# Probabilities times values in plain float32, each head in its own half of the array's columns

## Chip, cores and metric

One core of one Trainium2 chip runs the whole kernel as one launch. The metric is the device time of one execution in microseconds (us). Before the change it is 646.23 us, the median of three runs (646.15 to 648.87).

## What is computed

```python
def _attn_ref(q, k, v, n_sink, window):           # q, k, v: (2, 8, 768, 64) float32
    scores = scale * np.matmul(q, k.transpose(0, 1, 3, 2))
    keep = is_sink | in_window                    # key < n_sink (4), or 0 <= query - key < window (128)
    scores = np.where(keep, scores, -1e9)
    a = np.exp(scores - np.max(scores, axis=-1, keepdims=True))
    a = a / (np.sum(a, axis=-1, keepdims=True) + 1e-09)
    return np.matmul(a, v)
...
x = attn_out, heads side by side                  # (1536, 512)
h = (x @ w1) * (x @ w2) @ w3 @ w_out              # 512 -> 1024 -> 1024 -> 512
g = max(h2, 0) + alpha * min(h2, 0),  h2 = h @ w_in   # 512 -> 2048
return g @ w_out2                                 # 2048 -> 512
```

## The kernel before

Matrix products that need full precision are made from single-pass float32r matmuls: each operand is split into a high part (a float32r copy, by ScalarE) and a low part (the rest, by VectorE), and three products of parts are added. The helper is `evac_split` (lines 243 to 245). Its copy and its subtraction stand in the profile under L244 and L245 for every stage that uses it.

The program has two stretches. **Attention** goes over 8 units (batch b, pair of heads hp). One unit has two heads (e = 0, 1) and six blocks of 128 queries (i). A block needs 272 keys at most: its own 128, the 128 before it, and 16 sink columns. Per block, `stage_S` makes the scores of both heads on TensorE (L415: per head three products, each on 64 of the array's 128 rows, the two heads alternating), VectorE masks and takes the maximum (L422), ScalarE makes the exponentials and their sum (L424), VectorE inverts the sum (L426, L427), and GpSimd scales the probabilities (L429) and gathers the sink columns (L433, L435). `stage_X` transposes the probabilities on TensorE (L450, g = 0, 1, 2 has two blocks each) and evacuates them. `stage_K` does so for the sink columns (L467, L468). `stage_Tq` and `stage_Tk` transpose q and k of the next unit (L375, L384). The **feed-forward stretch** begins inside the last unit with `stage_B` (L567) and then runs to the end.

`stage_V` multiplies probabilities by values. It makes a tile of 128 rows (64 per head) by 512 queries (m = 0) or 256 queries (m = 1). Key block j gives to the queries of blocks j and j+1, so to 256 columns, or to 128 at the edge of a tile and of the sequence. Blocks 0, 1, 2 and 4 (SPLIT) have high and low parts of both operands: values in `vp` (made by GpSimd in `split_v`, L364 and L365), probabilities in `PT` (made by `evac_split`, L244 and L245). Blocks 3 and 5 (WHOLE) are plain float32, values in `vw` (loaded by two further DMAs, L359), probabilities in `PW` (L456, L459). Each head's 64 value columns stand beside 64 zero columns, so a matmul is 128 columns wide and both heads add into all 128 rows of the tile. All matmuls of `stage_V` are recorded under L498:

```python
for vt, pt in ((vp[0], th), (vp[0], tl), (vp[1], th)):                    # SPLIT: three products
    ops.append((x0 - lo_col, x1 - lo_col, vt[:, n, c], pt[:, 2 * n * P:2 * n * P + w]))
...
ops.append((x0 - lo_col, x1 - lo_col, vw[u % 2][:, n, c], PW[e][:, y0:y0 + w]))     # WHOLE: one
```

By the loops, a unit has 24 products of parts 256 wide, 6 plain products 128 wide, and 2 products with the sink values (96 rows deep, 256 wide).

The order of work on each engine comes from a scheduler. Each stage is recorded at a position (table `OFF`: for unit u, 6u plus the offset, in blocks of scores), and the scheduler then orders the engines' instructions by its own estimates. `tc.high_priority()` puts what it encloses ahead of others, and `tc.issue_after` keeps an instruction behind another one. All input DMAs are issued on SP's queue. `bank(kind="V")` is one PSUM bank, `kind="T"` three; the scores have two pairs.

Of the kernel before, what the change touches and what calls it, by code (L numbers as in the profile page):

```python
# [196 lines left out]
def kernel(  # L197
# [119 lines left out]
    SPLIT, WHOLE = (0, 1, 2, 4), (3, 5)
    vp = [at(t2, n * len(SPLIT) * 3 * D, [len(SPLIT), 3 * D]) for n in range(2)]
    vw = [at(e2, 3840 + n * len(WHOLE) * 3 * D, [len(WHOLE), 3 * D]) for n in range(2)]
    vv = [t.rearrange("p n (c d) -> p n c d", d=D)[:, :, 0:3:2, :] for t in vp]  # L320

# [16 lines left out]
    def sink_values(b):  # L338
# [6 lines left out]
        for e in range(2):  # L345
# [5 lines left out]
            for n, (nm, m) in enumerate((("q", 0), ("q", 1), ("k", 0), ("k", 1), ("v", 0)))}  # L351
# [16 lines left out]
    qT = [[at(set1, n * S, [S]) for n in range(2)], [at(t2, 2 * len(SPLIT) * 3 * D, [S]), at(t1, 0, [S])]]  # L368
# [101 lines left out]
    def stage_V(u, m, e):  # L470
        b, hp = divmod(u, NP)
        lo_col, hi_col = ((0, 512), (512, S))[m]
        if e == 0:
# [4 lines left out]
        c = slice(e * D, e * D + P)
        for j in range(NB):
            a0, a1_ = j * P, min((j + 2) * P, S)  # L480
            x0, x1 = max(a0, lo_col), min(a1_, hi_col)
            if x0 >= x1:
                continue
            w = x1 - x0
            if j in SPLIT:
                n = SPLIT.index(j)
                for vt, pt in ((vp[0], th), (vp[0], tl), (vp[1], th)):
                    ops.append((x0 - lo_col, x1 - lo_col, vt[:, n, c], pt[:, 2 * n * P:2 * n * P + w]))
            else:
                n = WHOLE.index(j)  # L490
                y0 = 2 * n * P + x0 - a0
                ops.append((x0 - lo_col, x1 - lo_col, vw[u % 2][:, n, c], PW[e][:, y0:y0 + w]))
        if e == 1:
            x0 = max(2 * P, lo_col)
            ops.append((x0 - lo_col, hi_col - lo_col, vsk[b][:, hp].rearrange("p e d -> p (e d)"),
                        skT[:, x0 - 2 * P:hi_col - 2 * P]))
        for n, (x0, x1, lt, rt) in enumerate(ops):
            nc.tensor.matmul(xp[:, x0:x1], lt, rt, start=(e == 0 and n == 0), stop=(e == 1 and n == len(ops) - 1),  # L498
                             skip_group_check=True)
        if e == 1:  # L500
            o = slice(b * S + lo_col, b * S + hi_col)
            evac_split(xh[:, hp, o], xl[:, hp, o], xp)
# [158 lines left out]
    def masks_2():  # L661
        count(cols[2][:, P:KW], 1)
        for t in vw:
            nc.gpsimd.memset(t[:, :, D:2 * D], 0.0)
        for t in vp:
            nc.gpsimd.memset(t[:, :, D:2 * D].bitcast(F32), 0.0)
# [292 lines left out]
```

## Time and profile before

| | |
|---|---|
| median of 3 runs | 646.23 us |
| the profiled execution: its own time | 648.56 us |
| its span, first to last instruction | 646.4 us |
| TensorE (PE) busy | 630.1 us, 97% of the span |
| VectorE (DVE) / ScalarE (ACT) / GpSimd (POOL) busy | 57% / 43% / 24% |
| chain that ended last, by engine | PE 81%, DVE 6%, POOL 4%, DMA 3% |
| mean granted TensorE clock | 0.99 of full speed |

PE is busy nearly everywhere, but PE's busy time counts the modelled ends of pipelined matmuls, so what one matmul costs is read from starts that follow each other, and from the chain. The other three engines do most of their work in the first 150 us: a mean over the span hides that they are nearly as full as PE there. PEld is PE's weight load.

### The profile page before, as it was taken

To read this page: it belongs to the slowest core of one execution; us is meant where nothing else is said; L and a number is where in the kernel's file an instruction comes from. 1 tells how busy PE (TensorE), PEld (TensorE's weight loads), DVE (VectorE), ACT (ScalarE), POOL (GpSimd) and SP (SyncE) were. 2 spreads that over 40 slices of the span, in tenths; PEclk is the share of its full clock that TensorE was granted. 3 is DMA by queue.
4 is the path that set the end of the run, shared out by engine and by line. 5 is a ranking of instruction groups with operands and counts; after the bars stand their busy time and mean duration, and the time that the engine had idled before them with its cause. 6 is when DMAs were issued, how large, how long until landed. Compare 5 with 4: busy or idle time off the path is not lost.

```text
span 646.4 us, 8934 instructions
## 1 busy us (share of the span) xinstructions
PE 630.1 (97%) x3194; PEld 519.8 (80%) x3194; DVE 370.8 (57%) x778; ACT 281.0 (43%) x570; POOL 153.3 (24%) x281
## 2 busy tenths in 40 slices
PE   8899998999999999999999999999999999999995
PEld 5678887888888888888888887788888888888884
DVE  7898999778995656475454778922232222322222
ACT  4788888577765443354344555411111111111110
POOL 5768767500000000000000003422222222222220
PEclk9999999899999999999999999999999999999998
DMA  6834523255451223431105334100010000100002
GB/s 140 199 83 112 117 53 92 85 184 165 161 195 66 95 101 125 137 130 66 65 16 179 131 110 152 65 0 2 0 66 0 1 1 0 66 0 1 0 1 70
DMA packets 67687, 52.23 MB, mean 81 GB/s; under 512 B 44452, under 2 KB 61108, under 8 KB 67636
## 3 DMA queue, kind: packets, MB, share of 16 engines
q1 hardware_dynamic: 67344, 51.20, 26.1%
q8 instruction: 27, 0.44, 0.3%
q10 hardware_dynamic: 292, 0.39, 0.2%
q14 instruction: 24, 0.20, 0.1%
HBM read 48.44 MB, written 3.15 MB: 80 GB/s over the span
## 4 chain that ended last, share of the span: by engine, by line
PE 81%; DVE 6%; POOL 4%; DMA 3%; issue 3%; ACT 2%; SPq 0%; POOLq 0%; ACTq 0%; DVEq 0%
PE bank L567 20%; PE bank L893 18%; PE bank L878 17%; PE bank L841 9%; PE bank L531 7%; PE bank L498 4%; PE scores L415 2%; PE bank L450 2%; DVE RAW L422 2%; POOL T L251 1%; DVE EARLY L245 1%; PE bank L519 1%; DMA EARLY<-in_k_dram 1%; DMA RAW<-in_moe_w_out_dram 1%; DMA W3T<-in_moe_w_out_dram 1%
## 5 line engine op out<-in xcount | busy, mean ns | idle before, releaser
L251 POOL TENSOR_TENSOR T<-M,T 128x512 fp32r<-128x512 f32 x48 | 65.0, 1354 | 441.0 <-ACT T L250 441.0
L567 PE MATMUL bank<-X,SET 128*128 128x512 f32 x576 | 134.9, 392 | 0.4 <-DVE lim L757 0.4
L567 PEld LDWEIGHTS bank<-X,SET 128*128 128x128 f32 x576 | 107.0, 188 | 22.2 <-PE bank L450 0.6
L880 DVE TENSOR_SCALAR M<-bank,alpha_sb 128x512 f32<-128x512 f32 x48 | 36.0, 750 | 154.0 <-PE bank L878 152.8
L250 ACT ACTIVATE T<-M 128x512 fp32r<-128x512 f32 x48 | 30.3, 631 | 179.9 <-DVE M L881 178.4
L893 PE MATMUL bank<-EARLY,T 128*128 128x512 f32 x288 | 76.2, 390 | 0.8 <-ACT T L250 0.6
L878 PE MATMUL bank<-X,EARLY 128*128 128x512 f32 x288 | 74.2, 389 | 0.0
L893 PEld LDWEIGHTS bank<-EARLY,T 128*128 128x128 f32 x288 | 53.8, 188 | 13.0 <-ACT T L250 1.0
L878 PEld LDWEIGHTS bank<-X,EARLY 128*128 128x128 f32 x288 | 54.1, 188 | 11.2
L531 PE MATMUL bank<-LATE,W3T 128*128 128x512 f32 x192 | 45.6, 391 | 0.0
L235 DVE TENSOR_SCALAR CW<-CW 128x1024 f32<-128x1024 f32 (+1 forms) x37 | 25.3, 683 | 29.5 <-ACT CW L232 29.3
L531 PEld LDWEIGHTS bank<-LATE,W3T 128*128 128x128 f32 x192 | 35.8, 188 | 7.6
L893 PE MATMUL bank<-LATE,T 128*128 128x512 f32 x144 | 40.3, 390 | 0.3 <-POOL T L251 0.3
L878 PE MATMUL bank<-X,LATE 128*128 128x512 f32 x144 | 40.1, 389 | 0.0
L237 DVE SCALAR_TENSOR_TENSOR RAW<-RAW 128x1024 int32<-128x1024 int32 x20 | 25.0, 1249 | 26.0 <-ACT RAW L234 26.0
L422 DVE CUSTOM_DVE_ANT_0 RAW<-scores,EARLY 128x272 f32<-128x272 f32 (+1 forms) x96 | 36.6, 406 | 4.6 <-PE scores L415 3.6
L498 PE MATMUL bank<-EARLY,T 128*128 128x256 f32 x192 | 37.8, 318 | 1.0 <-ACT EARLY L244 0.6
L234 ACT ACTIVATE RAW<-RAW 128x1024 int32<-128x1024 uint8 x20 | 22.8, 1141 | 31.3 <-DMA RAW<-in_moe_w_out_dram 20.4
L841 PE MATMUL bank<-EARLY,T 128*128 128x512 f32 x144 | 34.6, 389 | 0.0
L232 ACT ACTIVATE CW<-RAW 128x1024 f32<-128x1024 f32 x20 | 22.8, 1140 | 26.7 <-DMA RAW<-in_moe_w_dram 17.9
L881 DVE SCALAR_TENSOR_TENSOR M<-bank,M 128x512 f32<-128x512 f32 x48 | 33.1, 689 | 1.3
L893 PEld LDWEIGHTS bank<-LATE,T 128*128 128x128 f32 x144 | 27.0, 188 | 6.3 <-POOL T L251 0.7
(174 smaller groups left out, 1084.9 us busy)
## 6 DMA issues: line engine op xcount, KB each, us to landing
RAW<-in_moe_w_dram SPq DMA_DIRECT2D x20, 512.0 KB, 4.5
ROW<-in_moe_w_dram SPq DMA_DIRECT2D x12, 512.0 KB, 4.9
RAW<-in_moe_w_out_dram SPq DMA_DIRECT2D x12, 512.0 KB, 4.6
RAW<-in_moe_w_in_dram SPq DMA_DIRECT2D x8, 512.0 KB, 3.9
W3T<-in_moe_w_in_dram SPq DMA_DIRECT2D x8, 512.0 KB, 3.7
W3T<-in_moe_w_out_dram SPq DMA_DIRECT2D x8, 512.0 KB, 4.6
RAW<-in_v_dram SPq DMA_DIRECT2D x16, 192.0 KB, 3.6
EARLY<-in_q_dram SPq DMA_DIRECT2D x14, 192.0 KB, 3.1
```

What stands on the lines that cost most here:

```text
L235: lambda: nc.vector.tensor_scalar(c.bitcast(F32), c.bitcast(F32), -LIMIT, LIMIT, ALU.max, ALU.min),
L250: nc.scalar.activation(hi, src, AF.Copy)
L251: nc.gpsimd.tensor_tensor(lo, src, hi.bitcast(F32), ALU.subtract)
L422: st["max", u, i] = nc.vector.tensor_tensor_reduce(sm[:, :w], ps[e][:, :w], masks[:, min(i, 2), SW - w:SW], -scale, 3.0e38, ALU.add, ALU.m ...
L498: nc.tensor.matmul(xp[:, x0:x1], lt, rt, start=(e == 0 and n == 0), stop=(e == 1 and n == len(ops) - 1), skip_group_check=True)
L531: nc.tensor.matmul(ps, l[:, c, :], rt[c], start=(n == 0), stop=(n == len(mm) - 1))
L567: nc.tensor.matmul(ps, l[:, n0 + c, :], r[:, c, o], start=(n == 0), stop=(n == len(mm) - 1))
L841: nc.tensor.matmul(ps, W(c, l)[:, m * P:(m + 1) * P], ab(c, t, r), start=(n == 0), stop=(n == len(mm) - 1))
L878: nc.tensor.matmul(ps, l[:, 0, c * P:(c + 1) * P], r[:, c, o], start=(m == 0), stop=(m == len(mm) - 1))
L880: nc.vector.tensor_scalar(g, ps, 0.0, alpha_sb[:, j:j + 1], ALU.min, ALU.mult)
L881: nc.vector.scalar_tensor_tensor(g, ps, 0.0, g, ALU.max, ALU.add)
L893: st["E"] = nc.tensor.matmul(acc[t][m], l[:, o], r[:, 1, :], start=(j == 0 and x == 0), stop=(j == KF2 - 1 and x == 2)).ins
```

## The change

`stage_V` now uses plain float32 for every key block. Head 0 writes rows 0 to 63 of the tile and head 1 rows 64 to 127, with 64 value columns as weights straight from the loaded values, and the heads' matmuls alternate. The sink product, all 128 columns wide, comes first and alone carries `start`. The probabilities' transposes are copied once, head 0's by ScalarE and head 1's by VectorE. `split_v`, `vp`, `vw`, `PW`, their zeroing and the second value loads are gone. The values of odd units have a place of their own (`EARLY2`), those of even units stay in `RAW`. The block is recorded under `high_priority` with each matmul behind the one before it.

```diff
     def load(u, nm, src):
         b, hp = divmod(u, NP)
         for e in range(2):
-            st["load"] = nc.sync.dma_start(raws[nm, u % 2 if nm != "v" else 0][:, :, e, :],
+            st["load"] = nc.sync.dma_start(raws[nm, u % 2][:, :, e, :],
                                            src[b, 2 * hp + e].rearrange("(n p) d -> p n d", p=P)).ins
-            if nm == "v":
-                nc.sync.dma_start(vw[u % 2][:, :, 2 * e * D:(2 * e + 1) * D],
-                                  src[b, 2 * hp + e].rearrange("(n p) d -> p n d", p=P)[:, 3::2, :])
-
-    def split_v(u, n):
-        o, src = ((slice(0, 2), slice(0, 2)), (slice(2, 4), slice(2, 5, 2)))[n]
-        nc.gpsimd.tensor_scalar(vv[0][:, o], raws["v", 0][:, src], 0.0, 1.0, ALU.add, ALU.mult)
-        nc.gpsimd.tensor_tensor(vv[1][:, o], raws["v", 0][:, src], vv[0][:, o].bitcast(F32), ALU.subtract)
...
-        if g == 0:
-            evac_split(th[:, 0:3 * P], tl[:, 0:3 * P], pt[:, 0:3 * P])
-        if g == 1:
-            evac_split(th[:, 3 * P:6 * P], tl[:, 3 * P:6 * P], pt[:, 0:3 * P])
-            nc.vector.tensor_copy(PW[e][:, 0:P], pt[:, 3 * P:4 * P])
-        if g == 2:
-            evac_split(th[:, 6 * P:8 * P], tl[:, 6 * P:8 * P], pt[:, P:3 * P])
-            nc.scalar.activation(PW[e][:, P:3 * P].rearrange("p (n c) -> p n c", c=P),
-                                 pt.rearrange("p (n c) -> p n c", c=P)[:, 0:4:3, :], AF.Copy)
+        o = max(4 * g - 1, 0) * P
+        dst = PT[e][:, o:o + n * P]
+        if e == 0:
+            nc.scalar.activation(dst, pt[:, 0:n * P], AF.Copy)
+        else:
+            nc.vector.tensor_copy(dst, pt[:, 0:n * P])
...
+        nc.tensor.matmul(xp[:, x0 - lo_col:], vsk[b][:, hp].rearrange("p e d -> p (e d)"),
+                         skT[:, x0 - 2 * P:hi_col - 2 * P], start=True, stop=False, skip_group_check=True)
         ops = []
         for j in range(NB):
...
+            x0, x1 = max(j * P, lo_col), min((j + 2) * P, hi_col)
+            for e in range(2):
+                if x0 < x1:
+                    ops.append((slice(e * D, (e + 1) * D), slice(x0 - lo_col, x1 - lo_col), raws["v", u % 2][:, j, e, :],
+                                PT[e][:, j * P + x0:j * P + x1]))
+        with tc.high_priority():
+            for n, (r, o, lt, rt) in enumerate(ops):
+                with tc.issue_after(st["V"]) if n else nullcontext():
+                    st["V"] = nc.tensor.matmul(xp[r, o], lt, rt, start=False, stop=n >= len(ops) - 2,
+                                               skip_group_check=True).ins
...
-    OFF = dict(X00=4.37, X10=4.92, X01=5.23, X11=4.69, K0=5.6, X02=6.73, V00=5.9, V01=7.05, X12=6.04,
-               K1=7.82, V10=8.21, V11=10.14, SV0=3.42, SV1=4.36, LV=1.95, Tk0=-3.59, Tk1=-3.67, Tq0=-3.17,
+    OFF = dict(X00=4.37, X10=4.92, X01=5.23, X11=4.69, K0=5.6, X02=6.73, V0=7.05, X12=6.04,
+               K1=7.82, V1=8.6, LV=1.95, Tk0=-3.59, Tk1=-3.67, Tq0=-3.17,
```

By the new loops a unit has, for both heads together, 8 plain products 256 wide, 6 plain products 128 wide, and the 2 sink products.

The order on PE around the products of unit 2, tile m = 0, while unit 3's last scores are made (before; L498 is `stage_V`, EARLY_0_79 and T_0_78 hold the parts, EARLY_0_81 the plain operands, EARLY_0_80 the sinks):

```order
L415 MATMUL scores_1017<-EARLY_0_80,T_0_78 128x272 x4
L450 MATMUL bank_905<-ident,W3T_89 128x128 x2
L450 MATMUL bank_905<-ident,M_90 128x128 x2
L498 MATMUL bank_871<-EARLY_0_79,T_0_78 128x256 x5
L498 MATMUL bank_871<-EARLY_0_81 128x128
L498 MATMUL bank_871<-EARLY_0_79,T_0_78 128x256 x9
L498 MATMUL bank_871<-EARLY_0_81 128x128
L498 MATMUL bank_871<-EARLY_0_80 128x256
L415 MATMUL scores_1069<-EARLY_0_80,ROW_0_85 128x272 x2
L415 MATMUL scores_1069<-EARLY_0_80,T_0_78 128x272 x4
```

Four more products of this tile stand earlier there, one, two and one at a time between scores and transposes. The same place after the change (L457 is the sink product, L469 the others; RAW holds the values; an output of 64 rows is one head):

```order
L434 MATMUL bank_812<-ident,M_90 128x128 x2
L401 MATMUL scores_921<-EARLY_0_80,ROW_0_85 128x272 x2
L401 MATMUL scores_921<-EARLY_0_80,T_0_78 128x272 x4
L401 MATMUL scores_959<-EARLY_0_80,ROW_0_85 128x272 x2
L401 MATMUL scores_959<-EARLY_0_80,T_0_78 128x272 x4
L457 MATMUL bank_833<-EARLY_0_80 128x256
L469 MATMUL bank_833<-EARLY_0_79,RAW_148 64x256 x6
L469 MATMUL bank_833<-EARLY_0_79,RAW_148 64x128 x2
L448 MATMUL bank_845<-ident,EARLY_0_81 96x128 x2
```

All products of the tile are one closed block now, behind the unit's last two blocks of scores, and no product stands between scores any more.

On POOL, between the sink columns of one unit and the scaling (L429) of the next one's probabilities, the splitting of the values (L364, L365) stood before:

```order
L364 TENSOR_SCALAR T_0_78<-RAW_148 128x2x2x64
L433 TENSOR_SCALAR EARLY_0_81<-M_90 128x2x32
L365 TENSOR_TENSOR T_0_78<-RAW_148,T_0_78 128x2x2x64
L435 TENSOR_TENSOR EARLY_0_81<-M_90,EARLY_0_81 128x2x16
L429 TENSOR_SCALAR T_0_88<-T_0_88,EARLY_0_81 128x128 x2
L429 TENSOR_SCALAR T_0_88<-T_0_88,EARLY_0_81 128x272 x2
L364 TENSOR_SCALAR T_0_78<-RAW_148 128x2x2x64
L365 TENSOR_TENSOR T_0_78<-RAW_148,T_0_78 128x2x2x64
```

and after the change:

```order
L419 TENSOR_SCALAR EARLY_0_81<-M_90 128x2x32
L421 TENSOR_TENSOR EARLY_0_81<-M_90,EARLY_0_81 128x2x16
L415 TENSOR_SCALAR T_0_88<-T_0_88,EARLY_0_81 128x128 x2
L415 TENSOR_SCALAR T_0_88<-T_0_88,EARLY_0_81 128x272 x4
L419 TENSOR_SCALAR EARLY_0_81<-T_0_88 128x2x32
```

Nothing stands between two scalings of one unit's probabilities now.

## Rows read from the trace of the kernel before

**Rows 1.** The page, part 1: busy time, share of the span, instructions.

```profile
PE 630.1 (97%) x3194; PEld 519.8 (80%) x3194; DVE 370.8 (57%) x778; ACT 281.0 (43%) x570; POOL 153.3 (24%) x281
```

**Rows 2.** Busy time by stretch, from one unit's first scores to the next unit's (units 3 to 6).

```profile
core 0: us, PE busy (x) PEld busy (x) DVE busy (x) ACT busy (x) POOL busy (x), PEclk, DMA share, GB/s
51.01:64.30 13.29, 13.29 (x113) 11.11 (x113) 11.72 (x51) 11.83 (x41) 10.41 (x28) 1.00 0.47 106
91.04:104.78 13.74, 13.31 (x112) 11.10 (x113) 12.58 (x53) 11.55 (x41) 12.11 (x32) 1.00 0.18 40
sum 53.77, PE 53.19 PEld 44.54 DVE 48.94 ACT 46.82 POOL 40.95; mean PE 13.30 PEld 11.14 DVE 12.24 ACT 11.70 POOL 10.24
```

**Rows 3.** The same view of unit 1, unit 7 and the first part of `stage_B`.

```profile
20.00:37.23 17.23, 15.09 (x116) 12.65 (x116) 13.77 (x56) 13.79 (x44) 11.61 (x32) 0.90 0.68 164
104.78:119.59 14.81, 12.79 (x86) 10.58 (x86) 10.91 (x46) 12.21 (x36) 9.20 (x21) 0.77 0.38 104
119.59:150.00 30.41, 30.41 (x171) 26.09 (x172) 26.20 (x48) 19.14 (x34) 4.94 (x11) 1.00 0.50 169
```

**Rows 4.** The chain that ended last: start us, us, what, xcount.

```profile
52.77 0.32 PE bank L498
...
53.86 0.23 PE bank L498 x2
...
57.46 2.23 PE bank L498 x19
59.69 0.58 PE scores L415 x6
...
61.81 1.95 PE bank L498 x15
...
87.98 0.70 POOL T L365
...
128.51 1.29 PE bank L498 x11
```

**Rows 5.** The timeline of PE: start us, us, what, shape, xcount.

```profile
129.42 0.38 PE L498 MATMUL bank<-EARLY 128*128 128x128 f32 x2
129.64 0.38 PE L450 MATMUL bank<-ident,W3T 128*128 128x128 f32 x2
```

**Rows 6.** L498 alone: duration ns min/median/max, first and last start, shape.

```profile
L498 PEld LDWEIGHTS bank<-EARLY,T x192: 186/192/333, 20.7 to 143.6; 128*128 128x128 f32 x192
L498 PE MATMUL bank<-EARLY x112: 270/275/553, 26.8 to 144.0; 128*128 128x128 f32 x96, 96*128 96x256 f32 x16
```

**Rows 7.** Groups by form from 51.01 to 104.78, DVE, ACT, POOL: busy us, mean ns.

```profile
L245 DVE TENSOR_TENSOR EARLY<-bank,EARLY 128x384 fp32r<-128x384 f32 x16 | 8.8, 551 | 0.2
L245 DVE TENSOR_TENSOR EARLY<-bank,EARLY 128x256 fp32r<-128x256 f32 x10 | 4.1, 415 | 0.1
L245 DVE TENSOR_TENSOR X<-bank,X 128x512 fp32r<-128x512 f32 x4 | 2.8, 688 | 0.9 <-ACT X L244 0.8
L456 DVE COPY EARLY<-bank 128x128 f32<-128x128 f32 x8 | 2.2, 280 | 0.0
...
L244 ACT ACTIVATE EARLY<-bank 128x384 fp32r<-128x384 f32 x16 | 7.7, 482 | 2.5 <-PE bank L450 2.5
L244 ACT ACTIVATE EARLY<-bank 128x256 fp32r<-128x256 f32 x10 | 3.8, 376 | 0.5 <-PE bank L450 0.5
L459 ACT ACTIVATE EARLY<-bank 128x256 f32<-128x256 f32 x8 | 2.8, 376 | 0.0
L244 ACT ACTIVATE X<-bank 128x512 fp32r<-128x512 f32 x4 | 2.4, 599 | 0.7 <-PE bank L498 0.7
...
L365 POOL TENSOR_TENSOR T<-RAW,T 128x256 fp32r<-128x256 f32 x8 | 5.8, 731 | 0.1
L364 POOL TENSOR_SCALAR T<-RAW 128x256 fp32r<-128x256 f32 x9 | 3.6, 402 | 3.3 <-DVE EARLY L245 3.2
```

**Rows 8.** DMA issues in the first 40 us: KB each, median us to landing.

```profile
EARLY<-in_v_dram SPq DMA_DIRECT2D x6, 64.0 KB, 2.7
```

More of the change, by code (lines that the diff above doesn't have):

```diff
@@ L312 @@
     t2 = place("T2", T2_WORDS, FR)
-    e0, e1 = (place(f"EARLY{n}", EARLY_WORDS, FR) for n in range(2))
+    e0 = place("EARLY0", EARLY_WORDS)
+    e1 = place("EARLY1", EARLY_WORDS, FR)
     e2 = place("EARLY2", EARLY_WORDS)
[L317 to L320, printed above, removed]
     RS = 6 * SK
@@ L350 @@
     raws = {(nm, m): at(e2, n * NB * 2 * D, [NB, 2, D])
-            for n, (nm, m) in enumerate((("q", 0), ("q", 1), ("k", 0), ("k", 1), ("v", 0)))}
+            for n, (nm, m) in enumerate((("q", 0), ("q", 1), ("k", 0), ("k", 1), ("v", 1)))}
     def load(u, nm, src):
@@ L355, in load @@
         for e in range(2):
-            st["load"] = nc.sync.dma_start(raws[nm, u % 2 if nm != "v" else 0][:, :, e, :],
+            st["load"] = nc.sync.dma_start(raws[nm, u % 2][:, :, e, :],
                                            src[b, 2 * hp + e].rearrange("(n p) d -> p n d", p=P)).ins
-            if nm == "v":
-                nc.sync.dma_start(vw[u % 2][:, :, 2 * e * D:(2 * e + 1) * D],
-                                  src[b, 2 * hp + e].rearrange("(n p) d -> p n d", p=P)[:, 3::2, :])
-    def split_v(u, n):
-        o, src = ((slice(0, 2), slice(0, 2)), (slice(2, 4), slice(2, 5, 2)))[n]
-        nc.gpsimd.tensor_scalar(vv[0][:, o], raws["v", 0][:, src], 0.0, 1.0, ALU.add, ALU.mult)
-        nc.gpsimd.tensor_tensor(vv[1][:, o], raws["v", 0][:, src], vv[0][:, o].bitcast(F32), ALU.subtract)
     t1, set1 = place("ROW0", QUARTER_WORDS, FR), place("SET1", SET_WORDS, FR)
-    qT = [[at(set1, n * S, [S]) for n in range(2)], [at(t2, 2 * len(SPLIT) * 3 * D, [S]), at(t1, 0, [S])]]
+    qT = [[at(set1, n * S, [S]) for n in range(2)], [at(t2, 0, [S]), at(t1, 0, [S])]]
     kT = [[at(t, o + n * NB * KW, [NB, KW]) for n in range(2)] for t, o in ((place("SET0", SET_WORDS, FR), 0), (e1, 0))]
@@ L437, in stage_S @@
         st[u, "P", i] = pe
-    PT = [[at(e0, (2 * e + n) * 1024, [8 * P]) for n in range(2)] for e in range(2)]
-    PW = [at(e2, 3072 + e * 384, [3 * P]) for e in range(2)]
+    PT = [at(e0, e * 2 * NB * P, [(2 * NB - 1) * P]) for e in range(2)]
     def stage_X(u, e, g):
-        th, tl = PT[e]
         pt = bank(kind="T")
@@ L468, in stage_K, with stage_V @@
         nc.scalar.activation(skT[:, 2 * m * P:2 * (m + 1) * P], pt[:RS, :2 * P], AF.Copy)
-    def stage_V(u, m, e):
+    def stage_V(u, m):
         b, hp = divmod(u, NP)
         lo_col, hi_col = ((0, 512), (512, S))[m]
-        if e == 0:
-            st["V", m] = bank(hi_col - lo_col, "V")
-        xp = st["V", m]
+        xp = bank(hi_col - lo_col, "V")
+        x0 = max(2 * P, lo_col)
+        nc.tensor.matmul(xp[:, x0 - lo_col:], vsk[b][:, hp].rearrange("p e d -> p (e d)"),
+                         skT[:, x0 - 2 * P:hi_col - 2 * P], start=True, stop=False, skip_group_check=True)
@@ L476, in stage_V @@
         ops = []
-        th, tl = PT[e]
-        c = slice(e * D, e * D + P)
         for j in range(NB):
[L480 to L502, printed above, removed]
+            x0, x1 = max(j * P, lo_col), min((j + 2) * P, hi_col)
@@ L505 @@
+        o = slice(b * S + lo_col, b * S + hi_col)
+        evac_split(xh[:, hp, o], xl[:, hp, o], xp)
     w3_blocks = w3.rearrange("(r p) (g f) t -> r p g f t", p=P, f=DM)
@@ L625 @@
     ns_ap, win_ap = eff[:, 0:1], eff[:, 1:2]
-    masks_r = at(e0, 4 * 1024, [3, SW])
-    masks = masks_r.bitcast(F32)
+    masks = at(e0, 4 * 1024, [3, SW])
     rel, keep, col0 = (at(t, 2 * SW, [SW]) for t in quarters)
@@ L638, in mask @@
     def mask(m, o, eng=nc.gpsimd):
-        nc.vector.scalar_tensor_tensor(masks_r[:, m, o], cols[m][:, o], ns_ap, keep[:, o], ALU.is_lt, ALU.max)
-        eng.tensor_scalar(masks_r[:, m, o], masks[:, m, o], -1.0, BIG, ALU.add, ALU.mult)
+        nc.vector.scalar_tensor_tensor(masks[:, m, o], cols[m][:, o], ns_ap, keep[:, o], ALU.is_lt, ALU.max)
+        eng.tensor_scalar(masks[:, m, o], masks[:, m, o], -1.0, BIG, ALU.add, ALU.mult)
     def kept(o):
@@ L662, in masks_2 @@
         count(cols[2][:, P:KW], 1)
[L663 to L666, printed above, removed]
         with tc.issue_after(st["max", 0, 1]):
@@ L717 @@
         elif nm[0] == "V":
-            stage_V(*arg, int(nm[1]), int(nm[2]))
-        elif nm[:2] == "SV":
-            split_v(*arg, int(nm[2]))
+            stage_V(*arg, int(nm[1]))
         elif nm[:2] == "Tk":
```

## Prediction, made before the changed kernel was run

> **What bounds the kernel now.** I read the page's busy line first: PE is busy 97% of the span and every other engine at most 57% [rows 1]. That mean says nothing about the change, whose work lies in the first 145 us, so I went to the stretches. In units 3 to 6 a unit takes 53.77 / 4 = 13.44 us, and PE is busy 13.30 of it, DVE 12.24, ACT 11.70, POOL 10.24 [rows 2]. So attention is bound by PE with three engines close behind; whoever is relieved alone gains little. In unit 6 the margin is thinnest, with DVE at 12.58 and POOL at 12.11 of 13.74. Unit 1 has PE busy 15.09 of 17.23 us and unit 7 12.79 of 14.81, so both are partly bound by something else, and their granted clock is 0.90 and 0.77; from 119.59 us on PE has no gap [rows 3]. The chain that ended last agrees: it runs through products of L498 on PE in the middle units, and through POOL's splitting of the values at 87.98 us [rows 4].
>
> **What the products cost now.** Two plain 128-wide rows start 0.22 us before the row behind them, 0.11 each [rows 5]. The program has 6 x 8 = 48 plain products, and the trace has 96 rows of them [rows 6]: each is two rows, 0.22 us for 128 columns. The chain's piece of 11 rows takes 1.29 us [rows 4]; nine are products of parts, so one costs (1.29 - 0.22) / 9 = 0.119 us for 256 columns. By these prices a unit's products cost 24 x 0.119 + 12 x 0.11 + 2 x 0.12 (sinks, taken as a product of parts) = 4.42 us. The chain shows unit 2's products as pieces of 1, 2, 19 and 15 rows with 0.32 + 0.23 + 2.23 + 1.95 = 4.73 us [rows 4]; one row is not in it, 0.12, so 4.85 us. The 0.43 above the prices is the cost of single products scattered between scores.
>
> **What they cost after.** A plain row of 256 columns is not in the trace. Two rows of 128 columns are the nearest: a 256-wide row takes 0.22 us, a 256-wide product 0.44, if width counts as it does for products of parts. A unit then has 8 x 0.44 + 6 x 0.22 = 4.84 us of plain rows, if one runs after the other. The whole question is whether the two heads' rows, in different columns of the array, run at the same time. No product before uses half the columns. The nearest row is the scores: six 272-wide products on alternating halves of the array's rows take 0.58 us [rows 4], while six in a row would take 6 x 0.119 x 272 / 256 = 0.76. Three such products alone would take 0.38. So halves by rows do overlap, and the 0.20 left over is the price of going into and out of that arrangement. In the alternating order a head's two rows follow each other, so its second row can run beside the other head's first; after the first row every row has a partner. Bounds: 2.42 us (all overlapped) and 4.84 (none). I take 2.42, because the nearest row overlaps nearly fully.
>
> The new form is entered twice per unit (tiles m = 0 and m = 1), 2 x 0.20 = 0.40 us; the scattered products, and their 0.43, are gone. Sinks stay, 0.24. So PE's products take 2.42 + 0.24 + 0.40 = 3.06 us, 1.79 less per unit.
>
> The price 0.20 is a measured one. [...]
>
> **The other engines, per unit.** DVE loses four subtractions of 384 (0.551), two of 256 (0.415) and two copies of 128 (0.280), 3.59 us [rows 7]. It gets copies of 384, 512 and 512 columns. The only copy in the trace is 128 wide, so I price them as subtractions of that width, an upper bound: 0.551 + 2 x 0.688 = 1.93 [rows 7]. Net 1.66 less. ACT loses 4 x 0.482 + 2 x 0.376 + 2 x 0.376 = 3.43 us and gets 0.482 + 2 x 0.599 = 1.68, net 1.75 less [rows 7]. POOL loses 2 x (0.402 + 0.731) = 2.27 us [rows 7]. DVE's and ACT's rows partly overlap their neighbours, so the true relief is somewhat under these sums. SP loses two of four value loads per unit (64 KB, 2.7 us to landing [rows 8]); the DMA share is 0.47 at most in the middle units [rows 2], so I count nothing; if a load were late it would show as PE waiting for DMA. The values are now read by PE itself, so the load of unit u+2's values waits for PE's last product of unit u, not for POOL; with two places that is a whole unit early, nothing. The zeroing on POOL at the start goes; unit 1 has other waits, nothing.
>
> **Sum.** A unit's floors become PE 13.44 - 1.79 = 11.65, DVE 10.58, ACT 9.95, POOL 7.97 us: PE stays the longest, and no engine takes its place. A block now needs every transpose evacuated before it begins, and the scores behind it wait for the block, so I give back 0.4 us per unit and take 1.4 of the 1.79. The products of units 1 to 7 lie where PE is the bound or nearly (37 to 145 us): 7 x 1.4 = 9.8. Unit 0's lie in unit 1's stretch, bound elsewhere: 0.5, between 0 and 1.8. What follows at 145 us shifts as a whole, since PE has no gap there. Together 10.3 us of the profiled execution's 648.56: 638.3. That execution is 2.3 us above the median, 646.23; by the median the time is **636 us**. The two stretches with a lower clock I leave as they are; if the one in unit 7 went (14.81 x 0.23 = 3.4 us), the time would be lower by that.
>
> **Rivals.**
> - The halves do not overlap. Then products take 4.84 + 0.24 + 0.40 = 5.48 us, 0.63 more per unit, 7 x 0.63 = 4.4 in all: about 650. For it: no row of before uses column halves, and each half streams all 128 rows of its own operand, which the scores' halves do not. Against: the scores. It turns slower where the overlap saves less than 0.63 us of a unit's 4.84, so at under 13%. Chance 0.16.
> - The gain is eaten: the closed block waits for the evacuations, scores come late, DVE idles while PE multiplies, and PE's gaps lower the clock as in unit 7, where 2 us of gaps [rows 3] stand beside a clock of 0.77 (3.4 us). A gain of 10 less two or three such stretches is 0 to 3: about 645. For it: products between scores filled PE's waits before. Against: DVE, ACT and POOL get more room than PE. Chance 0.12.
> - Weight loads come into the open. A load takes 0.192 us [rows 6], longer than the 0.11 between rows, so loads run under matmuls now. If they did not with half columns, 28 rows x 0.19 = 5.3 us per unit would come on top of 5.48: +5.9 per unit, about 688. [...] By that rule this would happen already before; the trace contradicts it, hence a chance of 0.04.
> - My forecast, overlap whole or in greater part: 0.68.
>
> **How the numbers follow.** A measurement of this kernel tells about 0.5% from no change, 3.2 us, so "same" is 643.0 to 649.5. Faster: 0.68 and 0.02 of the eaten gain, 0.70. Same: 0.08 of the eaten gain and 0.04 of no overlap, 0.12. Slower: 0.12 of no overlap, 0.02 of the eaten gain, 0.04 of the loads, 0.18. The full 1.79 per unit, unit 0's 1.8 and the 3.4 of clock give 17.7 us, so the lower end is 628; the upper end, 649, takes in nearly all of the eaten gain and part of no overlap. The forecast's own range is 628 to 642.
>
> **What would show it.** Right: rows of the two heads start in pairs, 64-wide weights, a tile m = 0 (12 rows 256 wide, 4 rows 128 wide, 3.08 us in a row) taking about 1.6 us behind its sink; units of some 12 us; DVE's share of a unit falling with PE's. Wrong: that tile taking 3 us (no overlap), or units of 13.4 us with overlapped rows, where the wait ahead of the block or ahead of the next scores names the culprit.

## The result, and the profile after

The changed kernel takes **636.79 us** in the median of four runs (636.48 to 640.04), beside 646.38 us for the kernel before on the same chip: 0.9854 of it, 95% interval 0.9814 to 0.9894. On a second chip it took 636.87 us beside 647.65 (0.9835, 0.9814 to 0.9857). The forecast was 636.0, between 628 and 649. The profiled execution took 637.03 us with a span of 635.2, so the spans differ by 646.4 - 635.2 = 11.2 us, of which 2.3 belong to an execution of before that lies above its median.

The page's busy line of the kernel after, which answers to [rows 1], and the chain that ended last by engine (PE had 81% of it before):

```profile
PE 613.7 (97%) x3130; PEld 496.3 (78%) x3130; DVE 360.5 (57%) x738; ACT 272.1 (43%) x530; POOL 137.1 (22%) x245
PE 69%; DVE 11%; ACT 7%; DMA 6%; issue 4%; POOL 2%; SPq 1%; ACTq 0%; DVEq 0%; POOLq 0%
```

The shares of the span have hardly moved. What changed is seen in the stretches (columns as in [rows 2]): units 3 to 6 with their sum, then units 1 and 2 and the last unit's stretch, which answer to [rows 3], and, last, units 1 and 2 of before, from their first scores:

```profile
48.44:60.52 12.08, 11.09 (x105) 8.54 (x104) 10.86 (x46) 10.79 (x36) 7.44 (x22) 1.00 0.46 99
...
84.41:96.60 12.19, 11.02 (x106) 8.56 (x105) 11.20 (x49) 10.63 (x35) 8.75 (x24) 1.00 0.12 28
sum 48.16, PE 45.40 PEld 34.23 DVE 44.04 ACT 42.69 POOL 30.99; mean PE 11.35 PEld 8.56 DVE 11.01 ACT 10.67 POOL 7.75
...
20.50:33.95 13.45, 11.42 (x99) 8.09 (x99) 10.96 (x46) 11.56 (x37) 8.61 (x24) 1.00 0.77 186
33.95:48.44 14.49, 11.74 (x105) 8.60 (x106) 12.55 (x52) 11.29 (x38) 10.57 (x30) 1.00 0.37 78
...
96.60:112.10 15.50, 13.05 (x104) 9.45 (x104) 12.43 (x47) 12.66 (x36) 5.94 (x17) 0.89 0.34 95
```

```profile
21.04:37.23 16.19, 14.41 (x112) 12.07 (x111) 12.73 (x54) 13.78 (x44) 10.57 (x30) 0.89 0.64 158
37.23:51.01 13.78, 12.72 (x113) 10.97 (x112) 12.93 (x55) 11.99 (x41) 9.09 (x25) 1.00 0.40 91
```

A middle unit takes 48.16 / 4 = 12.04 us where it took 13.44 [rows 2], and PE is busy 11.35 of it where it was busy 13.30 of 13.44: PE now has gaps of 0.7 us a unit that it did not have. DVE, ACT and POOL are at 11.01, 10.67 and 7.75.

The 11.2 us by place, from the starts of the units in the two traces: unit 0, 21.04 - 20.50 = 0.5. Units 1 and 2 together (21.04 to 51.01 before, 20.50 to 48.44 after), 29.97 - 27.94 = 2.0. Units 3 to 6, 53.77 - 48.16 = 5.6. From unit 7's start to the end, (646.4 - 104.78) - (635.2 - 96.60) = 3.0.

The timeline of PE, one tile m = 0 (L457 is the sink product, L469 the two heads' rows):

```profile
66.23 0.38 PE L457 MATMUL bank<-EARLY 96*128 96x256 f32 x1
66.54 1.74 PE L469 MATMUL bank<-EARLY,EARLY 128*64 128x256 f32 x16
68.20 0.42 PE L448 MATMUL bank<-ident,EARLY 128*96 128x128 f32 x2
```

The 16 rows start within 68.20 - 66.54 = 1.66 us (1.74 counts the last one's modelled end). In the trace the heads' rows start in pairs, 6 ns apart, from the very first pair on. The second pair follows the first 0.267 us later, each further pair of 256-wide rows 0.216 us. L469 alone, both kinds of record, which answers to [rows 6]:

```profile
L469 PEld LDWEIGHTS bank<-EARLY,RAW x112: 132/137/232, 25.4 to 110.7; 128*64 128x64 f32 x112
L469 PE MATMUL bank<-EARLY,RAW x112: 272/379/635, 25.4 to 110.9; 128*64 128x256 f32 x64, 128*64 128x128 f32 x48
```

A weight load of 64 columns takes 0.137 us (0.192 for the 128 of L498 [rows 6]), and two of them lie under each pair: the loads for the next pair start 1 to 2 ns behind a pair's rows. Both heads' products use all 128 rows of the array (128*64 above), and the loads run under them. The rule to which the prediction points at its rival of the loads is shown by no run; the trace shows this overlap, and the rival that the loads come into the open is gone with it.

The copies in units 3 to 6 (groups by form, columns as in [rows 7]):

```profile
L441 DVE COPY EARLY<-bank 128x512 f32<-128x512 f32 x8 | 5.5, 685 | 0.2 <-PE bank L434 0.2
L441 DVE COPY EARLY<-bank 128x384 f32<-128x384 f32 x4 | 2.2, 548 | 0.0
...
L439 ACT ACTIVATE EARLY<-bank 128x512 f32<-128x512 f32 x8 | 4.6, 576 | 0.0
L449 ACT ACTIVATE EARLY<-bank 96x256 fp32r<-96x256 f32 x8 | 2.9, 364 | 0.0
```

A wide copy on DVE costs what a subtraction of its width cost in [rows 7] (0.688 and 0.551): what the forecast called an upper bound was the value.

Where PE's gaps come from: PE's waits in units 3 to 6 (us in total, times, longest), and the longest such wait of all, on PE's timeline at the end of unit 2 (in brackets the idle time before it):

```profile
PE bank L361 <- ACT EARLY L449: 2.2, 2, 1.2
PE bank L361 <- DVE SET L245: 0.3, 1, 0.3
...
45.95 0.66 PE L361 MATMUL bank<-ident,EARLY 128*128 128x128 f32 x4 [1.59 <-ACT EARLY L449]
```

L361 is the transpose of the next unit's queries. It needs one of the three `T` banks, and one of these holds the sink transposes until ACT has copied them (L449), behind exponentials and other copies in ACT's queue. In the same view of before PE waits 0.4 us in all in these units, once, for DVE.

### The profile page after: what moved, and what is told of

It is laid out like the page before. It is cut to its first block, busy times and chain, and to the rows that moved or that the text cites. A ratio compares the mean times of both kernels' runs of the same rounds, so it can differ in the third digit from the quotient of the medians.

```text
span 635.2 us, 8620 instructions
## 1 busy us (share of the span) xinstructions
PE 613.7 (97%) x3130; PEld 496.3 (78%) x3130; DVE 360.5 (57%) x738; ACT 272.1 (43%) x530; POOL 137.1 (22%) x245
## 4 chain that ended last, share of the span: by engine, by line
PE 69%; DVE 11%; ACT 7%; DMA 6%; issue 4%; POOL 2%; SPq 1%; ACTq 0%; DVEq 0%; POOLq 0%
PE bank L856 19%; PE bank L841 17%; PE bank L537 13%; PE bank L804 9%; PE bank L501 6%; DVE CW L238 2%; DMA ROW<-in_moe_w_dram 2%; POOL T L251 2%; DMA ROW<-in_moe_w_out_dram 2%; DVE RAW L408 2%; ACT W3T L410 1%; PE bank L469 1%; DVE EARLY L245 1%; ACT T L410 1%; PE bank L489 1%
## 5 line engine op out<-in xcount | busy, mean ns | idle before, releaser
L856 PE MATMUL bank<-EARLY,T 128*128 128x512 f32 x288 | 76.3, 390 | 0.4 <-POOL T L251 0.4
L856 PEld LDWEIGHTS bank<-EARLY,T 128*128 128x128 f32 x288 | 53.9, 188 | 12.4 <-POOL T L251 1.2
L841 PEld LDWEIGHTS bank<-X,EARLY 128*128 128x128 f32 x288 | 54.1, 188 | 11.2
L856 PE MATMUL bank<-LATE,T 128*128 128x512 f32 x144 | 40.3, 390 | 0.4 <-POOL T L251 0.4
L237 DVE SCALAR_TENSOR_TENSOR RAW<-RAW 128x1024 int32<-128x1024 int32 x20 | 25.0, 1250 | 25.8 <-ACT RAW L234 25.7
L232 ACT ACTIVATE CW<-RAW 128x1024 f32<-128x1024 f32 x20 | 22.8, 1142 | 25.6 <-DMA RAW<-in_moe_w_dram 18.1
L856 PEld LDWEIGHTS bank<-LATE,T 128*128 128x128 f32 x144 | 27.0, 188 | 6.4 <-POOL T L251 0.8
L804 PEld LDWEIGHTS bank<-EARLY,T 128*128 128x128 f32 x144 | 27.0, 188 | 5.6
```

The costliest lines, as they stand in the source:

```text
L237: lambda: nc.vector.scalar_tensor_tensor(low, high, -0x80000000, low, ALU.bitwise_and, ALU.bitwise_or),
L804: nc.tensor.matmul(ps, W(c, l)[:, m * P:(m + 1) * P], ab(c, t, r), start=(n == 0), stop=(n == len(mm) - 1))
L841: nc.tensor.matmul(ps, l[:, 0, c * P:(c + 1) * P], r[:, c, o], start=(m == 0), stop=(m == len(mm) - 1))
L856: st["E"] = nc.tensor.matmul(acc[t][m], l[:, o], r[:, 1, :], start=(j == 0 and x == 0), stop=(j == KF2 - 1 and x == 2)).ins
```

## The experiments

The runs stand in four groups, each beside the kernel before on the same chip (medians 647.32, 647.65, 647.44 and 645.89 us), so ratios are what is compared across groups: 0.001 of them is 0.65 us. To follow PE, I sum for units 3 to 6, by line, the time from each PE row's start to the next row's start, and divide by four; the sum is the unit. A wait thus counts with the row ahead of it.

| us of PE per unit | before | full width | heads in turn | after |
|---|---|---|---|---|
| products with values and sinks (L498; L457, L469, L470) | 5.15 | 5.25 | 4.49 | 3.39 |
| scores (L415; L401) | 3.39 | 2.98 | 3.04 | 3.06 |
| transposes of probabilities (L450; L434) | 2.69 | 2.74 | 2.81 | 2.83 |
| transposes of q and k (L375, L384; L361, L370) | 1.62 | 1.44 | 1.59 | 2.19 |
| transposes of sinks (L467; L448) | 0.59 | 0.51 | 0.57 | 0.57 |
| unit | 13.44 | 12.92 | 12.50 | 12.04 |

**The heads one after the other**

```diff
-        for j in range(NB):
-            x0, x1 = max(j * P, lo_col), min((j + 2) * P, hi_col)
-            for e in range(2):
+        for e in range(2):
+            for j in range(NB):
+                x0, x1 = max(j * P, lo_col), min((j + 2) * P, hi_col)
```

> The changed kernel with one edit: head 0's products of a tile all come before head 1's, so nothing runs in the other column half. Every other row stands where it stood on each engine. Theory (the gain is the overlap of the heads' rows on PE): a tile m = 0 takes about 3.1 us behind its sink where it took 1.6, products cost 2.42 us more per unit, a unit goes from 12.0 to about 14.0 us and the time to 636.8 + 7 x 2.0 = about 651 us, no faster than before the change. Rival (the gain is the work taken off DVE, ACT and POOL, and PE had room): under 640 us.

Measured: 639.03 us, ratio 0.9866 (0.9841 to 0.989), far under what I expected. The changed kernel has 0.9854 and 0.9835, so this run is 0.8 to 2 us above it, and the intervals overlap. The edit did not remove the overlap. L469 alone in three stretches of one tile (m = 0; PE and PEld busy with the number of rows in each stretch, then clock, DMA share and GB/s):

```profile
67.19:68.11 0.92, 0.91 (x4) 0.60 (x5) 1.00 0.00 0
68.11:68.67 0.56, 0.56 (x8) 0.51 (x7) 1.00 0.15 29
68.67:69.70 1.03, 1.03 (x10) 0.62 (x6) 1.00 0.00 0
```

A row that runs on from one stretch into the next counts in both, so by starts these are 4, 7 and 5 rows. Four rows of head 0 run alone; head 1's first row then starts 6 ns behind head 0's fifth (its load, which alone waits for DVE's copies, starts in the trace at 68.121, beside it), ahead of head 0's sixth, seventh and eighth; the last five run alone. The tile's 16 rows take 69.78 - 67.20 = 2.58 us. So here a row for the other column half starts ahead of three rows that stand before it in the program.

**Full width: no overlap**

```diff
-                    ops.append((slice(e * D, (e + 1) * D), slice(x0 - lo_col, x1 - lo_col), raws["v", u % 2][:, j, e, :],
+                    ops.append((slice(0, P), slice(x0 - lo_col, x1 - lo_col),
+                                raws["v", u % 2][:, j].rearrange("p e d -> p (e d)"),
```

> Every product of the block takes the values of both heads as 128-wide weights and writes all 128 rows of the tile, so that two rows can never share the array; number, order and column counts of the rows stay. The output then mixes the heads' sums in each row: it is no longer the attention product. My theory (the gain on TensorE is the overlap of the two heads): the twelve 256-wide and four 128-wide rows of tile m = 0 take about 3.1 us in place of 1.7, a unit's rows 4.84 in place of about 2.7 us, so units of 3 to 6 of about 13.7 us in place of 12.04, and 646 to 651 us in all. Rival 1 (the relief of VectorE, ScalarE and GpSimd and the new order carry the gain, the overlap is worth little): at most 641 us with units under 12.8. Rival 2 (from the run with the heads one after the other, where the end was only 2 us later: the tail takes most of any loss back): units of 13.7, but under 643 us.

Measured: 643.04 us, ratio 0.993 (0.9908 to 0.9951), so 6.2 us above the changed kernel beside it and 4.6 under the kernel before. The same tile on PE's timeline, and the sum of units 3 to 6:

```profile
66.97 0.39 PE L457 MATMUL bank<-EARLY 96*128 96x256 f32 x1
67.19 3.20 PE L470 MATMUL bank<-EARLY,EARLY 128*128 128x256 f32 x16
70.32 0.39 PE L401 MATMUL scores<-SET,SET 64*128 64x272 f32 x2
```

```profile
sum 51.70, PE 51.53 PEld 44.54 DVE 44.39 ACT 43.23 POOL 33.68; mean PE 12.88 PEld 11.13 DVE 11.10 ACT 10.81 POOL 8.42
```

The rows take 70.32 - 67.19 = 3.13 us, as the theory said, against 1.66: the overlap makes them 1.9 times as fast. But the unit grows by 0.89 us only, not by 1.7. The table shows both halves of that: products cost 1.86 us more (5.25 against 3.39), while the transposes of q and k cost 0.75 less (1.44 against 2.19), since PE no longer waits at them (PE is busy 51.53 of 51.70 us). And this kernel, whose products cost PE as much as before (5.25 against 5.15), is still faster than before. So the overlap, with what it costs to go in and out of it, is worth 6.2 us, and 4.6 come without it.

Part of the 4.6 may be the clock. The nine executions of the kernel before on this chip have mean granted clocks from 0.989 to 0.998, and the two highest (0.997 and 0.998) took 645.99 and 646.02 us, 1.6 less than the median; all four at full width have 0.996 to 0.998. Beside those two the gain without overlap is 3.0 us. No run separates the clock from PE's waits in the same stretches. In the middle units the clock is 1.00 in both traces, so their 4 x 0.52 = 2.1 us are not the clock's.

**What the other engines' relief is worth**

Relief alone, in the kernel before: the low parts are not made, and the products of parts read the high parts in their place, so PE does the same work in nearly the old order. `evac` is one copy, head 0's on ACT, head 1's on DVE.

```diff
-        nc.gpsimd.tensor_tensor(vv[1][:, o], raws["v", 0][:, src], vv[0][:, o].bitcast(F32), ALU.subtract)
...
-            evac_split(th[:, 0:3 * P], tl[:, 0:3 * P], pt[:, 0:3 * P])
+            evac(th[:, 0:3 * P], pt[:, 0:3 * P])
...
-                for vt, pt in ((vp[0], th), (vp[0], tl), (vp[1], th)):
+                for vt, pt in ((vp[0], th), (vp[0], th), (vp[0], th)):
```

> The kernel before with the relief alone: the low parts of probabilities and values are not made (the high parts stand in for them in the products, so the output lacks the low parts), head 0's transposes are evacuated by ACT and head 1's by DVE; PE has the same products as before. Per unit DVE has some 1.4 us less, ACT 1.4, POOL 1.5. Theory (PE bounds a unit at 13.3 of 13.4 us): 643 to 646 us, the few us from units 1, 6 and 7, where PE had waits. Rival (the relief carries the gain): about 638 us.

Measured: 644.29 us, ratio 0.9957 (0.9941 to 0.9972): a gain of 3.0 us, 4.1 between the two profiled spans. By place, unit 0 loses 0.3, units 1 and 2 gain 3.7 (29.97 us before), the middle units lose 0.9 (53.77 before), and the part from unit 7's start on (from 102.34 and 104.78 us) gains 1.6. So the middle units have none of the gain, and in units 1 and 2 the clock is 1.00 where it was 0.94 over both. Units 1 and 2, then 3 to 6:

```profile
21.37:47.66 26.29, 25.10 (x217) 21.26 (x216) 22.82 (x99) 22.85 (x78) 17.26 (x49) 1.00 0.64 145
47.66:102.34 54.68, 51.71 (x449) 44.44 (x449) 46.06 (x195) 43.33 (x150) 36.34 (x104) 1.00 0.35 77
```

The other way round, relief taken back in the changed kernel, on DVE (subtractions for head 0, into an unused place, 1.93 us a unit by the prices of [rows 7]) and on POOL (the splitting of the values, 2.27 us):

```diff
+            nc.vector.tensor_tensor(at(e0, 3072, [n * P]), pt[:, 0:n * P], dst, ALU.subtract)
```

> The changed kernel with DVE's relief undone: for head 0 the transposed probabilities are also subtracted on DVE, into a place that nobody reads, 384 + 512 + 512 columns per unit, about 1.93 us where the relief was 1.66. PE's products are untouched. Theory (PE's saving is the cause, but DVE at 10.9 of 12.0 us per unit is close behind): DVE's 12.8 us becomes the unit's floor, +0.5 to +0.9 us per unit, 640 to 643 us. Rival (overlap alone carries the gain, DVE's relief is idle time): 636 to 638 us. Other rival (the relief carries it): 645 us or more.

```diff
+    def split_v(u, n):
+        src = raws["v", u % 2][:, 2 * n:2 * n + 2]
+        nc.gpsimd.tensor_scalar(pool_back[0], src, 0.0, 1.0, ALU.add, ALU.mult)
+        nc.gpsimd.tensor_tensor(pool_back[1], src, pool_back[0], ALU.subtract)
```

> The changed kernel with POOL's splitting of the values put back, into a place that nobody reads: 4 instructions, 2.27 us per unit. Theory: POOL has 7 to 9 busy us of a unit of 12.0, so nothing moves, 636 to 638 us. Rival (the splitting stood in front of the scaling of the probabilities in POOL's queue and its removal was part of the gain): 639 us or more.

Measured: 638.87 us, 0.9864 (0.9844 to 0.9884), and 639.07 us, 0.9868 (0.9849 to 0.9887). By the ratios that is 0.6 to 2.1 us above the changed kernel, with intervals that overlap its own, so at the end neither loss is clear of noise; the stretches show more. Units 3 to 6 of the first in sum, and its unit 1:

```profile
sum 50.63, PE 47.46 PEld 34.06 DVE 49.09 ACT 43.81 POOL 32.84; mean PE 11.87 PEld 8.51 DVE 12.27 ACT 10.95 POOL 8.21
```

```profile
20.50:35.85 15.35, 13.52 (x102) 9.25 (x102) 13.48 (x53) 12.44 (x39) 9.77 (x28) 0.89 0.61 153
```

DVE is now busy 12.27 us of a unit of 50.63 / 4 = 12.66, 0.62 more than after. So with the overlap on PE, DVE stands at the bound; without its relief a third of the 1.93 us shows in the unit, and part of the overlap's gain needs the relief to show. (The added subtraction also keeps the transposes' bank for longer, as the subtraction of before did; this run does not tell the two apart.) With POOL's splitting taken back, units 3 to 6 last from 48.75 to 98.44 us, 12.42 a unit and 0.38 more than after: the expectation that nothing moves was wrong there, though POOL was the least busy engine.

**The wait at the sink columns**

```diff
-        nc.scalar.activation(skT[:, 2 * m * P:2 * (m + 1) * P], pt[:RS, :2 * P], AF.Copy)
+        nc.vector.tensor_scalar(skT[:, 2 * m * P:2 * (m + 1) * P], pt[:RS, :2 * P], 0.0, 1.0, ALU.add, ALU.mult)
```

> The changed kernel with the sink columns' evacuation on VectorE in place of ScalarE, where it stands behind exponentials and other evacuations while the tile that it reads holds one of three banks. Theory (what the block gives back per unit is this wait: TensorE waits 4.8 us at the next unit's query transposes and 1.9 at a probability transpose for it): these waits go, 1 to 4 us less than the changed kernel beside it, 633 to 636. Rival (the bank is given free earlier, but VectorE, with 10.8 us of a 12.0 us unit busy, holds up the scores instead): no difference within 0.3%, or up to 2 us slower, with TensorE waiting for VectorE there.

and, beside it, the changed kernel once more:

> The changed kernel itself once more, as the base for the three runs beside it and for the earlier ones: 636.8 us, within 0.3%.

Measured: 636.95 us, 0.985 (0.9825 to 0.9875), beside 636.87, 0.9835 (0.9814 to 0.9857): no difference. Yet the wait on ACT is gone, and unit 7 starts at 95.12 us in place of 97.07: 1.95 us ahead. Nearly all of it comes from unit 2 (12.49 us in place of 14.50). In the middle units PE waits for DVE instead, and they take 48.55 us in place of 48.21:

```profile
PE bank L457 <- DVE X L245: 1.1, 1, 1.1
PE bank L457 <- DVE EARLY L449: 0.4, 1, 0.4
PE bank L361 <- DVE SET L245: 0.4, 1, 0.4
```

The lead then melts in the feed-forward stretch. With as many PE rows still to come (3130 in all), the two traces stand 1.75 us apart at 2160 rows (139.97 and 141.72 us), 1.10 at 1800 (218.28, 219.38), 0.37 at 1600 and 0 at 500. PE's waits from 155 to 265 us, of this kernel, then of the changed one beside it:

```profile
PE bank L489 <- DVE CW L238: 1.6, 2, 1.1
```

```profile
PE bank L489 <- DVE CW L238: 0.5, 2, 0.3
```

L489 transposes a weight block, L238 is the last of the five steps (L232 to L238, two on ACT, three on DVE) that decode it. The longer of the two ends at 171.3 us. The chain of waits ahead of it (start us, us, what) goes through a loop: a load lands, is decoded, that frees its place, and only then the next load goes out.

```profile
145.88 4.90 DMA ROW<-in_moe_w_dram
...
150.80 1.14 ACT ROW L234
...
151.97 1.23 DVE ROW L237
153.19 1.15 DVE CW L238
...
154.81 4.62 DMA RAW<-in_moe_w_dram
...
160.69 1.23 DVE RAW L237
```

From 160.69 us on DVE has no gap, and the L238 that PE waits for stands behind other work in its queue (timeline of DVE):

```profile
166.57 1.21 DVE L237 SCALAR_TENSOR_TENSOR ROW<-ROW 128x1024 int32<-128x1024 int32 x1
167.71 1.27 DVE L543 TENSOR_TENSOR M<-bank,M 128x512 f32<-128x512 f32 x2
168.91 1.21 DVE L245 TENSOR_TENSOR SET<-CW,SET 128x1024 fp32r<-128x1024 f32 x1
170.04 1.21 DVE L238 SCALAR_TENSOR_TENSOR CW<-CW,ROW 128x1024 int32<-128x1024 int32 x1
```

So what was said ahead of the change, that DVE and ACT do most of their work in the first 150 us, does not hold: in the trace of before DVE has 127.5 of its 370.8 us there and ACT 115.3 of 281.0. The decoding of weights keeps DVE as full beyond: 67.1 of the 78 us from 112 to 190 us in the changed kernel's second trace.

**The decoding held back**

```diff
...
-            with tc.issue_after(st["max", NU - 1, 5]):
+            with tc.issue_after(st["max", NU - 1, 5]), tc.issue_after(st["exp", NU - 1, 5]):
                 load12(1)
```

> The changed kernel with the second weight decode of the feed-forward stretch held behind the last unit's last exponential on ScalarE; all else as it is. Theory (of the lead of 13.5 us at the last scores, 2.2 us are lost because ScalarE decodes weights for 2.3 us, after a wait of 0.9 us for their load, ahead of the last exponentials, which leaves TensorE a gap of 2.2 us and then the lower clock for 3.4 us): gap and low clock at 108 us go, the lead at the end grows by 1 to 2 us, 634.5 to 636 us. Rival (the decode was needed that early: the feed-forward stretch now waits for its weights): gap moves behind 112 us, no difference within 0.3% or slower.

Measured: 638.33 us (635.79 to 640.01), 0.9852 (0.9826 to 0.9879): not distinguishable from the changed kernel. The gap at 108 us went, and the profiled execution, one of the two slowest of five, paid for it later: it is 3.7 us ahead of the changed kernel's first trace at 2300 rows to come and 3.7 behind at 1600, with a span of 638.1 us. Its longest waits from 100 us on:

```profile
PE bank L489 <- DVE CW L238: 3.9, 2, 3.1
```

So the rival held: the decoding was needed that early. The low clock that I wanted to remove was worth nothing at the end: in the second trace of the changed kernel the last unit's stretch has a clock of 1.00, and its span is 635.1 us beside 635.2. On the way it was worth something. The second trace is 0.47 us behind the first at 2400 rows to come, 1.63 ahead at 2300, just after the stretch with the low clock, 0.44 ahead at 1800 and level at 1600: this lead, too, melts in the feed-forward stretch.

```profile
97.07:112.50 15.43, 13.68 (x113) 10.09 (x113) 13.28 (x50) 13.15 (x37) 6.00 (x17) 1.00 0.38 108
```

**Is it the decoding that takes further gains?** First by giving DVE room: the weights' low parts on POOL, which is busy 4.75 of the 78 us from 112 to 190 us in the changed kernel's second trace; alone, and with the sink columns on DVE.

```diff
-        split(h_, l_, c.rearrange("p (k f) -> p k f", f=P))
+        (split_pool if f else split)(h_, l_, c.rearrange("p (k f) -> p k f", f=P))
...
-            split(woh[n + m], wol[n + m], c[:, m * DM:(m + 1) * DM])
+            split_pool(woh[n + m], wol[n + m], c[:, m * DM:(m + 1) * DM])
```

> The changed kernel with the low parts of the feed-forward weights (of load12 from the second on, and of wout) made on GpSimd in place of VectorE; attention as it is. GpSimd has nothing to do there, VectorE is busy 12 to 15.5 us of each 16 between 112 and 190 us, mostly with decoding weights, and TensorE waits for that decoding at 160 and 172 us (about 0.5 us each) in the changed kernel. Theory (from some 11 us of gain on, the decoding of weights on VectorE, not attention, sets when TensorE goes on): VectorE gets 10 us of room, the two waits go, 0.5 to 1.5 us less than the changed kernel: ratio 0.981 to 0.983. Rival (GpSimd, 1.43 us for 512 columns where VectorE takes 0.69, delivers the parts too late): 1 to 4 us slower, with TensorE waiting for GpSimd.

> The run before it with the sink columns' evacuation on VectorE besides, which by itself brought attention 1.5 to 2 us ahead and the end nothing (0.9850 beside 0.9835 for the changed kernel). Theory (that gain was lost at VectorE's decoding of weights, at 171 and 243 us): with room on VectorE it now reaches the end, 1 to 2 us less than the run before it. Rival (it was lost elsewhere: in the loads of the weights, 4.6 us each through two places, or in the rows of TensorE themselves): the two runs agree within 0.2%.

Measured: 644.22 us, 0.9956 (0.9939 to 0.9974), and 639.71 us, 0.9889 (0.9864 to 0.9913). The first lost 7 us. PE's longest wait there:

```profile
PE bank L537 <- DVE M L543: 3.6, 1, 3.6
```

It ends at 164 us, and from 163.98 to 167.40 us the granted clock is 0.50 (0.83 in the mean of 160 to 170 us). The shift to POOL (2.63 us for a part that takes DVE 1.22) also moved DVE's order, and this pair is no clean test, though the lead of attention did reach the end in it (the second is 4.5 us under the first). A cleaner one shortens the decoding by L237, the second of DVE's three steps, so that the weights lose their signs:

```diff
-        decode(c, raw)
+        decode(c, raw, slice(0, 3)); decode(c, raw, slice(4, 5))
```

> The changed kernel with one of the five steps of every weight decode of the feed-forward stretch left out, VectorE's third (1.22 to 1.25 us for 1024 columns, the weights' signs); so the weights are all positive there and the result is not the reference's. Attention is as it is. Theory (from some 11 us of gain on, the decoding of weights sets when TensorE goes on): TensorE's waits for decoded weights at 160 and 172 us (0.5 us each) go; 0.5 to 2 us less than the changed kernel, ratio 0.980 to 0.983. Rival (they are the loads' waits, or the new order costs as much): within 0.3% of the changed kernel's ratio, 0.9835.

> The run before it, with the same step left out, and with the sink columns' evacuation on VectorE besides, which by itself brought attention 1.5 to 2 us ahead and the end nothing. Theory (that lead was lost at the decoding of weights): with shorter decoding it reaches the end, 1 to 2.5 us less than the run before it. Rival (lost elsewhere): the two runs agree within 0.15%.

Measured: 634.05 us, 0.9815 (0.9793 to 0.9836), and 631.27 us, 0.9767 (0.9744 to 0.979). With shorter decoding the edit of the sink columns is worth 2.8 us; with the whole decoding it was worth nothing. PE's gaps from 112 to 190 us are gone in both. The stretch, of the kernel with the sinks on DVE, then of the same with the shorter decoding:

```profile
112.00:190.00 78.00, 76.74 (x371) 62.16 (x370) 66.15 (x93) 50.78 (x69) 4.73 (x8) 1.00 0.46 153
```

```profile
112.00:190.00 78.00, 78.00 (x378) 63.49 (x377) 52.96 (x73) 50.64 (x69) 0.97 (x4) 1.00 0.47 161
```

The shorter decoding alone is not clear of the changed kernel (0.9815 beside 0.9835, intervals overlap), and its gain lies mostly elsewhere than I expected. It is 1.0 us ahead of the changed kernel's second trace at 1600 rows to come (262 us) and 3.6 at 500 (511 us). Between these two the changed kernel's PE waits 1.3 us for POOL (L856, four times), and in this run PE has no such wait. Decoding goes on until 403 us in the changed kernel, but why POOL is late there no run shows. No version of the whole computation beats the changed kernel here.

## Why the prediction was right, step by step

- **"What the products cost now", 4.85 us a unit.** 5.15 from start to start in units 3 to 6, 0.3 more than the chain had for unit 2's products.
- **"Its second row can run beside the other head's first; after the first row every row has a partner".** Right, and one row better: the first has its partner too. The tile took 1.66 us (about 1.6 forecast). Bounds were 2.42 and 4.84 for the rows; measured 2.77 with the way in and out, and 4.81 at full width.
- **"The new form is entered twice per unit", 0.40.** Sinks cost 0.62 instead of 0.44 at full width, and rows 2.77 instead of 2.42; together 0.53.
- **"3.06 us, 1.79 less per unit".** 3.39, and 1.76 less than the 5.15.
- **"I give back 0.4".** Net 0.36: transposes of q and k +0.57, of probabilities +0.14, scores -0.33, sinks -0.02. The place was misnamed. I had the block and the scores behind it wait; they did not. The wait is one stage later, at a bank that ACT frees late, and PE alone pays it.
- **What this sum hid.** It reads as if PE's saving were the gain, less a small loss. By the runs the overlap saves PE 1.86 us a unit and 0.89 arrives, and 0.52 arrives with no saving on PE (13.44 to 12.92). The two errors, 0.52 that was put at nothing and a give-back of 0.4 where 1.86 - 0.89 = 0.97 is lost, cancel: that the unit came out at 1.40 beside 1.4, and the time within 1 us, is luck in that part. Of the 0.52, 0.41 lie in the scores' rows (3.39 to 2.98), between which no product stands any more; that this order is the cause is not shown.
- **"The halves do not overlap", about 650.** This rival's condition was tried, and its PE time was right (5.48 forecast, 5.25 measured), but the time is 643.0, faster than before. The step that fails is 0.63 a unit more on a unit of 13.44: it kept before's unit, which is 0.52 shorter here though nothing overlaps.
- **Unit 0's 0.5, and 1.4 for unit 2's stretch.** Units 1 and 2 gave 2.0 against 1.9, but unit 1 gave 2.7 and unit 2 lost 0.7, so the agreement is luck. The two stretches with a lower clock "I leave as they are": in unit 1 the low clock went, and that decided nothing there: with relief taken back on DVE it came again (0.89 in the row above), and both units took 27.91 us together, beside 27.94. In the last unit it came in one trace of the changed kernel and not in the other, with equal spans. For the kernel before, whose executions at the higher clocks are the faster ones, it is open.
- **"What follows at 145 us shifts as a whole".** True for what this change gains, and for losses (full width: 6.25 us late at 2200 rows to come, 6.11 at 500), but not for more: the decoding of weights is the next bound, and the changed kernel already touches it (0.5 us of waits in its second trace, none in its first).
- **DVE 10.58, ACT 9.95, POOL 7.97.** 11.01, 10.67 and 7.75. "PE stays the longest, and no engine takes its place" holds for the sum, but DVE is so near that 1.93 us on it cost 0.62.

What stays open: how the 4.6 us that come without the overlap split into relief, order and clock. Relief alone gave 3.0, in the old order and outside the middle units; the closed block alone, with the old parts, was not tried.

## What to carry to other kernels

Two plain float32 products that each fill half the array's output columns ran side by side here, with their rows in alternation: 0.216 us for a pair of 256-wide rows, and 1.66 us for a tile that took 3.13 at full width. Price such a pair as one row, and add some 0.26 us per visit for going in and out (0.53 for the two visits of a unit here). Where three engines are within 15% of each other, ask of each saving how much room the others have, since the same saving was worth 1.86 us on its engine and 0.89 in the unit. And when an edit shortens a stage without shortening the kernel, compare the time at which equally many rows are left: it shows where the lead goes.

## What the runs showed of the hardware

- Matmul rows for the other half of the columns start ahead of earlier rows in the program (with the heads in turn, four rows run alone, then head 1's first, its load at 68.121 us, starts 6 ns behind head 0's fifth and ahead of its sixth, seventh and eighth).
- Weight loads of 64 columns take 0.137 us and lie under running rows (the loads for the next pair start 1 to 2 ns behind a pair's rows, 0.216 us ahead of their own); both heads' products use all 128 rows of the array.
- A plain float32 row of 256 columns alone takes 0.22 us (with the heads in turn, head 0's fourth row starts at 67.90 us and its fifth at 68.12), twice a row of 128 (0.11 [rows 5]), and a pair in two halves takes 0.216.
